# Addresses of the matrix-product operands: one distance modulo 256 bytes between what streams and what is loaded, by padded blocks and unused bytes

## The chip, the cores and the metric

One core of one Trainium2 chip runs the whole kernel in one launch. The metric is the device time in microseconds. An execution is a fixed program on five engines: PE (matrix products), ACT, DVE and POOL (element-wise work), and SP, which in this kernel issues most of the DMAs. On PE a matrix product is two records: a weight load (PEld), which puts 128 columns of the stationary operand into the array, and the matmul itself (PE), which streams the moving operand past them.

## The reference

```
h  = x + softmax_attention(layernorm(x) @ wqkv) @ wo      # 2048 x 512, 32 heads of 16
z  = gelu(layernorm(h) @ w_in)                            # 2048 x 1376
z1, z2 = z[:, :688], layernorm(z[:, 688:])
g  = w_sp @ z2 + b_sp[:, None]                            # 2048 x 2048 by 2048 x 688
out = h + (z1 * g) @ w_out                                # 688 x 512
```

All of it is float32 in and out. S is 2048, D is 512, FH is 688, FC = FH // 2 is 344.

## The kernel before

Nearly every product is made in three passes over a number split in two parts (`hi` and `lo`, both of type F32R): `mm3` issues `hi*hi`, `hi*lo` and `lo*hi` one behind the other into one PSUM accumulator, which are the lines L85, L86 and L87 of the profile. In a PE row the first name behind the arrow is the operand that streams, the second the one that is loaded: in `acc<-xT,wqk` xT streams and wqk is loaded, in `acc<-wv,xT` wv streams and xT is loaded, in `g<-t,ws` (and `g<-b,ws`, `g<-n,ws`) a block of z2 streams and a block of w_sp, `ws`, is loaded, in `acc<-wi,hT` wi streams, in `acc<-wo,o` wo, in `acc<-wu,pT` wu.

The kernel has four stages. Within each the order on PE, ACT, DVE and SP is written out by hand, from the last three stages on POOL's too.

1. **Projections.** x is normalised and transposed to `xT`; `proj_v` (wv streams, 512 columns) and `proj_qk` (xT streams, 512 columns) make v, q and k, which go to DRAM. From the fourth group of the second block on, five matmuls of the row maxima (`max_pair`, L214) stand inside each `proj_qk`.
2. **Attention.** Eight head groups; for each, 16 key blocks by 4 query blocks. PE makes scores (L647), row maxima of later rows (L214) and the weighted sum (L658); ACT takes the exponential; DVE takes the maxima. The keys `kst` of even head groups lie in a pool at one end of the memory, those of odd ones in a pool at the other end. Meanwhile `load_weights` brings wo and w_in in through a staging tile `wg` and POOL splits them into `wo2` and `wi2`.
3. **Mid stage.** For each of 16 row blocks: `make_h` (wo streams, 512 columns), `turn` (transposes into hT), and four calls of `make_z`, one for each quarter of w_in, 12 matmuls of 344 columns each, then gelu and layernorm. `gate_z` also makes the four blocks `t3`, `t2`, `n4` and `t1` of combinations of z2, each 8 by 344 numbers in a partition.
4. **Final stage.** w_sp @ z2 by seven block products of half the size in place of eight (as Strassen and Winograd have it). Each `product` is 24 matmuls of 344 columns (8 blocks by three passes). Four products for each of 8 row blocks p first (g7, g6, g4, g5), whose sums `q` go to DRAM, then three for each p (g1, g3, g2), the gate, the transposes `tp<-ident,pr` and the last product (wu streams, 512 columns, 18 matmuls for each output block).

Blocks that stream in the stages 3 and 4 are rows of 344 numbers that lie end to end:

```
wi2 = [ec.tile([P, DB, 2 * FH], F32R, name=f"wi{i}") for i in range(2)]
T = {n: [zc.tile([P, HB, FC], F32R, name=f"{n}_{i}") for i in range(2)]
     for n in ("t3", "t2", "n4", "t1")}
```

344 numbers are 1376 bytes, that is 5 * 256 + 96. A loaded block is 128 numbers, 512 bytes. So with each step to the next row the start of what streams moves by 96 bytes against the start of what is loaded, modulo 256. Tiles are put into memory one behind the other, from the left end or (side="right") from the right end, in the order in which their pools are opened; sizes are rounded up to 32 bytes.

Of the kernel before, what the change touches and what calls it, by code (L numbers as in the profile page):

```python
# [8 lines left out]
F32 = mybir.dt.float32  # L9
F32R = mybir.dt.float32r  # L10
# [8 lines left out]
P = 128  # L19
S = 2048  # L20
D = 512
H = 32
DH = 16
FH = 688
# [3 lines left out]
HB = NB // 2  # L28
NQ = S // 512
DB = D // P  # L30
# [7 lines left out]
VW = DH + 1  # L38
FB = [min(i * P, FH - P) for i in range(6)]
FC = FH // 2  # L40
LOW = -3.0e38


@with_exitstack
def block_kernel(ctx: ExitStack, tc: tile.TileContext, x, wqkv, wo, w_in, w_sp4, b_sp, w_out, out):
# [7 lines left out]
    nc = tc.nc  # L53
    E = mybir.EngineType

    const = ctx.enter_context(tc.tile_pool(name="const", bufs=1))
# [2 lines left out]
    make_identity(nc, ident)  # L59
    bias = const.tile([P, NB], F32, name="bias")  # L60
    nc.gpsimd.dma_start(bias, b_sp)

    q_scr = dram.tile([2, H * DH, S], F32, name="q_scr")
    k_scr = dram.tile([2, H * DH, S], F32, name="k_scr")
# [72 lines left out]
    qst, mx, turned = {}, {}, {}  # L137
# [118 lines left out]

    with ExitStack() as pre:
        p2 = pre.enter_context(tc.tile_pool(name="pre_2", bufs=2))
        pc = pre.enter_context(tc.tile_pool(name="pre_c", bufs=1))
        pt = pre.enter_context(tc.tile_pool(name="pre_pt", bufs=2, space=PSUM))  # L260
        ps = [pre.enter_context(tc.tile_pool(name=f"pre_ps{i}", bufs=2 - i, space=PSUM))
# [182 lines left out]
        with tc.manual_schedule(engines={E.PE, E.Activation, E.DVE, E.SP}):  # L444
# [43 lines left out]
            for g in range(3):  # L488
                a, b = 4 * g, 4 * g + 4
# [44 lines left out]
            for j in range(24):  # L534
                b, n, i = 1 + j // 8, j // 2 % 4, 1 - j % 2
# [28 lines left out]
    wc = late.enter_context(tc.tile_pool(name="wc", bufs=1))  # L564
    e2 = late.enter_context(tc.tile_pool(name="early_2", bufs=2))
    early = ctx.enter_context(ExitStack())
    ec = early.enter_context(tc.tile_pool(name="early_c", bufs=1))
    wo2 = [wc.tile([P, DB, D], F32R, name=f"wo{i}", tag=f"w{1 + i}") for i in range(2)]
    wi2 = [ec.tile([P, DB, 2 * FH], F32R, name=f"wi{i}") for i in range(2)]
    wo4 = wo.rearrange("(a p) c -> p a c", p=P)  # L570
    wi4 = w_in.rearrange("(a p) c -> p a c", p=P)

# [56 lines left out]
    with ExitStack() as at:  # L629
# [43 lines left out]

        def load_weights(i):

            t = wc.tile([P, DB * D], F32, name="wg", tag="w0")
            if i < 2:
                t = t[:, :2 * D].rearrange("p (a c) -> p a c", a=2)
                a, f = slice(2 * i, 2 * i + 2), slice(0, D)
                src, dst = wo4, wo2  # L680
            else:
                t = t[:, :2 * FH].rearrange("p (a c) -> p a c", a=2)
                b = FH * (i // 4)
                a, f = slice(i % 2 * 2, i % 2 * 2 + 2), slice(b, b + FH)
                src, dst = wi4, wi2
            nc.sync.dma_start(t, src[:, a, f])
            split(dst[0][:, a, f], dst[1][:, a, f], t, "pool", "pool")
# [134 lines left out]
    with ExitStack() as mid:  # L822
        m2 = mid.enter_context(tc.tile_pool(name="mid_2", bufs=2))
        zs, zst = {}, {}
        ph = mid.enter_context(tc.tile_pool(name="mid_ph", bufs=1, space=PSUM))
        pt = mid.enter_context(tc.tile_pool(name="mid_pt", bufs=2, space=PSUM))
        ps = mid.enter_context(tc.tile_pool(name="mid_ps", bufs=5, space=PSUM))

        def turn(sb):
# [11 lines left out]

        def make_z(sb, i, c):

            hT, f = hTs[sb], slice(i * FH + c * FC, i * FH + (c + 1) * FC)
# [81 lines left out]

    with ExitStack() as fin:
        bc = fin.enter_context(tc.tile_pool(name="fin_b", bufs=1, side="right"))
        fs = fin.enter_context(tc.tile_pool(name="fin_s", bufs=1, side="right"))
        fq = fin.enter_context(tc.tile_pool(name="fin_q", bufs=1, side="right"))  # L930
        f1 = late.enter_context(tc.tile_pool(name="fin_1", bufs=2))
# [36 lines left out]
        for p in range(HB):  # L968
            nxt, new, last = {}, [old[2], old[3], now[0], now[1]], p + 1 == HB
            ahead = p + 2 if p + 2 < HB else None  # L970
            g7, g6, g4, g5 = [next_g() for _ in range(4)]
            p6, p67 = [f1.tile([P, FC], F32, name=n) for n in ("p6", "p67")]
            q = [(fq if last else f1).tile([P, FC], F32, name=f"q{i}") for i in range(3)]

            def keep(i, g, other):
                nc.vector.tensor_add(q[i], g, other)
# [30 lines left out]
            if not last:  # L1007
                nxt["a22"] = put(new[2], a22)

                if ahead:  # L1010
                    a11 = ask(0, 0, ahead, "xr")
                else:
                    s2 = half("s4", "xr", 3)
                    for n in range(2):
                        nc.sync.dma_start(s2[n], cut(s_scr[0])[n])
                a22 = ask(1, 1, ahead, "o") if ahead else ask(0, 1, 0, "o")
            else:

                b22 = [zc.tile([P, HB, FC], F32R, name="b22", tag=f"t3_{i}") for i in range(2)]
                b21 = []  # L1020

                def put_next(b, k):
                    put_b(b, k, bs.pop(0))
                    if asked:
                        bs.append(load_b(*asked.pop(0)))

                for k in range(6):
                    put_next(b22, k)
                combine(nc.vector, s2, a22, s2, ALU.subtract)
                s4 = put(f[1], s2)  # L1030
                for k in range(6, HB):
                    put_next(b22, k)
# [3 lines left out]
            if not last:  # L1036
                nxt["s1"] = put(new[3], a21)
                if ahead:
                    a21 = a
                else:  # L1040
                    a11 = a
                b = load_b(0, 0, p + 1)
                if not ahead:
                    asked = [(1, 1, k) for k in range(HB)] + [(1, 0, k) for k in range(HB)]
                    bs = [load_b(*asked.pop(0)) for _ in range(5)]
            else:
                a12 = put(f[2], a22)
                b21 = [zc.tile([P, HB, FC], F32R, name="b21", tag=f"t2_{i}") for i in range(2)]
# [16 lines left out]
            keep(1, g4, p67)  # L1065
            product(g5, ops["s1"], T["t1"])
            if last:
                t = zc.tile([P, HB * FC], F32, name="qz", tag="t1_1")
# [11 lines left out]
        t = zc.tile([P, HB * FC], F32R, name="wu5", tag="t1_0")  # L1080
        for i, places in enumerate([[w[:, 2 * i:2 * i + 2, :] for w in wu] for i in range(2)]
                                   + [[w[:, 4, :] for w in wu], [t[:, j * D:(j + 1) * D] for j in range(2)]]):
            parts(*places, raw_u[i])
# [157 lines left out]
```

## Time and profile before

| | |
|---|---|
| median of 3 runs | 1884.37 us (1884.22 to 1887.94) |
| the profiled execution: its time, its span | 1884.14 us, 1882.3 us |
| granted PE clock | 1.00 |
| PE busy in the span | 1870.1 us, 99% |
| matmuls in the profile | 11606 |

How to read it: the span goes from the first to the last instruction; 1.8 us of the execution lie around it. A matmul's record has a modelled end and overlaps the record of the next one, so the length of a record is not what it costs. What it costs is the distance from its start to the start of the next: where rows of the timeline follow each other without a wait, the first start, the last start and the count give the mean cost of one.

### The profile page before, as it was taken

Reading aid. Unit: us, or ns where it says so; the run is one execution under the profiler, and the core shown is the slowest. Engines: PE = TensorE matmul, PEld = TensorE weight load, DVE = VectorE, ACT = ScalarE, POOL = GpSimd, SP = SyncE. Lnnn points to the kernel's source line nnn. Section 1 sums busy time; section 2 is a strip of 40 time slices with the busy share of each in tenths; the row PEclk is TensorE's granted clock in tenths of the full one; section 3 lists DMA queues with packets and bytes.
Section 4 is the critical chain, followed back from the end, with each engine's and each line's share of the span. In section 5 each row is a group of like instructions: output and inputs, shape, how many; then the busy total and the mean of one; then the engine's idle time right before and its main releaser. Section 6 shows DMA issues by size and latency. Waiting matters only on the chain.

```text
span 1882.3 us, 32332 instructions
## 1 busy us (share of the span) xinstructions
PE 1870.1 (99%) x11606; PEld 1066.4 (57%) x11606; DVE 1526.9 (81%) x3044; ACT 1328.3 (71%) x1716; POOL 205.6 (11%) x288
## 2 busy tenths in 40 slices
PE   9999999999999999999999999999999999999999
PEld 6766444444444444444444444444438999999998
DVE  6487999999999999999999999999935666867554
ACT  3334888888888888888888888888885444434221
POOL 2130000011010100000000000000001756001111
PEclk9999999999999999999999999999999999999999
DMA  6677210221120111021012011100024555768562
GB/s 190 177 199 187 51 24 25 51 54 28 38 53 18 52 41 24 19 47 38 13 38 41 16 38 38 24 13 16 4 73 129 159 160 168 222 194 269 186 190 85
DMA packets 148392, 159.82 MB, mean 85 GB/s; under 512 B 62984, under 2 KB 93208, under 8 KB 146696
## 3 DMA queue, kind: packets, MB, share of 16 engines
q1 hardware_dynamic: 143448, 146.35, 28.8%
q10 hardware_dynamic: 4752, 11.41, 1.6%
q8 instruction: 91, 1.49, 0.3%
q14 instruction: 69, 0.57, 0.1%
q0 software_dynamic: 32, 0.01, 0.0%
HBM read 101.16 MB, written 55.61 MB: 83 GB/s over the span
## 4 chain that ended last, share of the span: by engine, by line
PE 96%; DMA 1%; DVE 1%; issue 1%; ACT 0%; SPq 0%; POOLq 0%; DVEq 0%; ACTq 0%
PE pv L658 27%; PE m L214 26%; PE s L647 13%; PE acc L85 6%; PE acc L87 6%; PE acc L86 6%; PE g L87 3%; PE g L85 3%; PE g L86 3%; PE tp L1125 0%; PE tp L834 0%; DMA h<-h_scr 0%; DMA a<-in_w_sp 0%; PE tp L214 0%; PE tp L355 0%
## 5 line engine op out<-in xcount | busy, mean ns | idle before, releaser
L650 ACT ACTIVATE pt<-s 128x1024 f32<-128x1024 f32 x1024 | 993.6, 1031 | 147.5 <-PE s L647 142.0
L219 DVE TENSOR_REDUCE mx<-m 128x1 f32<-128x512 f32 x1511 | 958.8, 684 | 106.9 <-PE m L214 67.3
L214 PE MATMUL m<-kst,qst 48*128 48x512 f32 x1511 | 607.5, 448 | 0.0
L658 PE MATMUL pv<-pt,vst 128*32 128x512 f32 x4096 | 550.2, 605 | 0.7 <-ACT o L665 0.7
L647 PE MATMUL s<-qst,kst 50*128 50x512 f32 x2048 | 466.2, 428 | 2.1 <-DVE part L82 1.5
L214 PEld LDWEIGHTS m<-kst,qst 48*128 48x128 f32 x1511 | 263.5, 184 | 315.8 <-DVE mx L219 221.6
L647 PEld LDWEIGHTS s<-qst,kst 50*128 50x128 f32 x2048 | 223.0, 185 | 57.1 <-ACT pt L650 31.4
L214 PE MATMUL m<-uvs,qst 48*128 48x512 f32 x503 | 249.1, 496 | 0.0
L214 PEld LDWEIGHTS m<-uvs,qst 48*128 48x128 f32 x503 | 91.8, 183 | 207.3 <-DVE mx L219 205.3
L228 DVE CUSTOM_DVE_ANT_0 ab<-m,ab 128x512 f32<-128x512 f32 x252 | 171.7, 681 | 4.0 <-PE m L214 2.1
L658 PEld LDWEIGHTS pv<-pt,vst 128*32 128x32 f32 x4096 | 82.9, 108 | 160.3 <-issue 154.6
L224 ACT ACTIVATE ab<-m 128x512 f32<-128x512 f32 x251 | 151.0, 602 | 16.5 <-PE m L214 16.2
L79 POOL CAST mparts<-nm 128x16 fp32r<-128x16 f32 x32 | 6.3, 198 | 911.1 <-DVE nm L234 911.1
L777 ACT ACTIVATE ws<-a 128x512 fp32r<-128x512 f32 x80 | 45.9, 622 | 54.3 <-PE g L87 27.6
L85 PE MATMUL acc<-wi,hT 128*128 128x344 f32 x256 | 83.1, 325 | 0.0
L87 PE MATMUL acc<-wi,hT 128*128 128x344 f32 x256 | 81.8, 319 | 0.0
L86 PE MATMUL acc<-wi,hT 128*128 128x344 f32 x256 | 81.7, 319 | 0.0
L849 ACT ACTIVATE z<-acc 128x344 f32<-128x344 f32 x64 | 29.2, 458 | 62.7 <-PE acc L87 56.0
L778 DVE TENSOR_TENSOR ws<-a,ws 128x512 fp32r<-128x512 f32 x80 | 56.6, 750 | 13.5 <-ACT ws L777 13.4
L85 PE MATMUL g<-b,ws 128*128 128x344 f32 x192 | 62.6, 326 | 0.0
L87 PE MATMUL g<-b,ws 128*128 128x344 f32 x192 | 61.3, 319 | 0.0
L85 PE MATMUL g<-t,ws 128*128 128x344 f32 x192 | 61.3, 319 | 0.0
(193 smaller groups left out, 2134.5 us busy)
## 6 DMA issues: line engine op xcount, KB each, us to landing
a<-in_w_sp SPq DMA_DIRECT2D x80, 256.0 KB
qst<-q_scr SPq DMA_DIRECT2D x192, 64.0 KB
kst<-k_scr SPq DMA_DIRECT2D x48, 256.0 KB
z_scr<-z ACTq DMA_DIRECT2D x32, 344.0 KB
k_scr<-part SPq DMA_DIRECT2D x16, 512.0 KB
q_scr<-part SPq DMA_DIRECT2D x16, 512.0 KB
z<-z_scr SPq DMA_DIRECT2D x14, 344.0 KB
b<-z_scr SPq DMA_DIRECT2D x24, 172.0 KB
```

The source lines that it names most:

```text
L85: nc.tensor.matmul(ps, lh, rh, start=first, stop=False)
L86: nc.tensor.matmul(ps, lh, rl, start=False, stop=False)
L87: nc.tensor.matmul(ps, ll, rh, start=False, stop=last)
L214: nc.tensor.matmul(acc, q[r, p, c], keys[r, p], start=True, stop=True)
L219: nc.vector.reduce_max(at(t, e if t else e - 1), acc, axis=AX.X)
L224: nc.scalar.activation(ab[0], acc, AF.Abs)
L228: nc.vector.tensor_tensor_reduce(ab[0], acc, ab[0], 0.5, LOW, ALU.add, ALU.max, at(0, 0))
L647: nc.tensor.matmul(s[:, t, :], k[r, p, kb * P:(kb + 1) * P], q[r, p, :], start=True, stop=True)
L650: nc.scalar.activation(t, s, AF.Exp, scale=DH ** -0.5)
L658: nc.tensor.matmul(pv[0][32 * j:32 * j + 32, :], vst[hg % 2][:, c:c + 32], pts[j % 2][:, j // 2, :], start=kb == 0, stop=kb == NB - 1)
L777: nc.scalar.activation(hi, src, AF.Copy)
L778: (nc.gpsimd if el == "pool" else nc.vector).tensor_sub(lo, src, hi.bitcast(F32))
```

## The change

It moves operands in memory and leaves the arithmetic, and the order of the instructions on PE, ACT, DVE and SP, as they are. The number that it sets is, for each kind of product, (address of the first byte that streams - address of the first byte that is loaded) modulo 256. In the two built programs:

| product | matmuls, columns | before | after |
|---|---|---|---|
| xT streams, wqk loaded | 384, 512 | 192 | 0 |
| wv streams, xT loaded | 192, 512 | 0 | 0 |
| wo streams, o loaded | 192, 512 | 0 | 0 |
| wi streams, hT loaded | 768, 344 | 0, 32, ... 224, 96 of each | 0 |
| t3, t2, n4, b11, b22, b21 stream, ws loaded | 1152, 344 | 0, 32, ... 224, an eighth each, moving by 96 from block to block | 64 |
| t1 streams, ws loaded | 192, 344 | the same | 64 and 192 in turn |
| wu streams, pT loaded | 288, 512 | 224 | 0 |
| scores, odd head groups (even: 0 in both) | 1024, 512 | 160 | 192 |
| maxima, odd head groups (even: 0 in both) | 1024, 512 | 96 | 64 |

The weighted sum of the attention (L658) has every multiple of 4 equally often in both.

To this end rows of 344 numbers get a pitch of 384 (1536 bytes, 6 * 256), those of t1 a pitch of 352; unused tiles (`gap`) of 224 and 64 bytes shift what follows; `wu` starts 16 numbers into its tile. To make room, and to place it, hT moves from its own double-buffered pool into one tile in the slot `w2` (as two halves taken in turn), wo2 goes to `w0` and `w1` and the staging tile to `w2`; p6, p67, q and one each of the two h and pr tiles of the final stage have one buffer in place of two. POOL splits w_in in pieces of one row (8 conversions and 8 subtractions in place of 4 and 4).

```diff
+PITCH = 384
+    def gap(pool, size):
+        if size:
+            pool.tile([P, size // 4], F32, name="gap")
+    gap(const, 224)
...
         p2 = pre.enter_context(tc.tile_pool(name="pre_2", bufs=2))
+        pg = pre.enter_context(tc.tile_pool(name="pre_g", bufs=1))
+        gap(pg, 64)
...
-    wo2 = [wc.tile([P, DB, D], F32R, name=f"wo{i}", tag=f"w{1 + i}") for i in range(2)]
-    wi2 = [ec.tile([P, DB, 2 * FH], F32R, name=f"wi{i}") for i in range(2)]
+    wo2 = [wc.tile([P, DB, D], F32R, name=f"wo{i}", tag=f"w{i}") for i in range(2)]
+    wi2 = [ec.tile([P, DB, 4, PITCH], F32R, name=f"wi{i}")[:, :, :, :FC] for i in range(2)]
...
-            t = wc.tile([P, DB * D], F32, name="wg", tag="w0")
+            t = wc.tile([P, DB * D], F32, name="wg", tag="w2")
...
+                for j in range(2):
+                    d = slice(a.start + j, a.start + j + 1)
+                    split(wi2[0][:, d, f], wi2[1][:, d, f], t[:, j:j + 1], "pool", "pool")
...
-    T = {n: [zc.tile([P, HB, FC], F32R, name=f"{n}_{i}") for i in range(2)]
+    NARROW = FC + 8
+    def quarter(pool, name, tag, pitch=PITCH):
+        return pool.tile([P, HB, pitch], F32R, name=name, tag=tag)[:, :, :FC]
+    T = {n: [quarter(zc, n, f"{n}_{i}", NARROW if n == "t1" else PITCH) for i in range(2)]
...
+        hT = wc.tile([P, 2, 2, DB, P], F32R, name="hT", tag="w2")
...
-            hTs[sb] = [m2.tile([P, DB, P], F32R, name=f"hT{i}") for i in range(2)]
+            hTs[sb] = [hT[:, i, turned[0] % 2] for i in range(2)]
+            turned[0] += 1
...
+        gap(fin.enter_context(tc.tile_pool(name="fin_g", bufs=1, side="right")), 64)
...
-        b11 = [bc.tile([P, HB, FC], F32R, name=f"b11_{i}") for i in range(2)]
+        b11 = [quarter(bc, "b11", f"b11_{i}") for i in range(2)]
...
-            p6, p67 = [f1.tile([P, FC], F32, name=n) for n in ("p6", "p67")]
-            q = [(fq if last else f1).tile([P, FC], F32, name=f"q{i}") for i in range(3)]
+            p6, p67 = [f1.tile([P, FC], F32, name=n, bufs=1) for n in ("p6", "p67")]
+            q = [fq.tile([P, FC], F32, name=f"q{i}") for i in range(3)]
...
-        wu = [zc.tile([P, HB * FC], F32R, name="wu", tag=f"n4_{i}")[:, :5 * D].rearrange(
+        off = 16
+        wu = [zc.tile([P, HB * PITCH], F32R, name="wu", tag=f"n4_{i}")[:, off:off + 5 * D].rearrange(
...
-            h = [f2.tile([P, D], F32, name=f"h{i}") for i in range(2)]
+            h = [f2.tile([P, D], F32, name=f"h{i}", bufs=2 - i) for i in range(2)]
...
-            top, bot = [Out(p + HB * i, h[i], f2.tile([P, FH], F32, name=f"pr{i}"))
+            top, bot = [Out(p + HB * i, h[i], f2.tile([P, FH], F32, name=f"pr{i}", bufs=2 - i))
```

More of the change, by code (lines that the diff above doesn't have):

```diff
@@ L674, in load_weights @@
         def load_weights(i):
-            t = wc.tile([P, DB * D], F32, name="wg", tag="w0")
+            t = wc.tile([P, DB * D], F32, name="wg", tag="w2")
+            a = slice(i % 2 * 2, i % 2 * 2 + 2)
             if i < 2:
                 t = t[:, :2 * D].rearrange("p (a c) -> p a c", a=2)
-                a, f = slice(2 * i, 2 * i + 2), slice(0, D)
-                src, dst = wo4, wo2
+                nc.sync.dma_start(t, wo4[:, a, :])
+                split(wo2[0][:, a, :], wo2[1][:, a, :], t, "pool", "pool")
             else:
                 t = t[:, :2 * FH].rearrange("p (a c) -> p a c", a=2)
[L683 to L687, printed above, removed]
+                b = i // 4
+                nc.sync.dma_start(t, wi4[:, a, FH * b:FH * b + FH])
+                t = t.rearrange("p a (b c) -> p a b c", b=2)
+                f = slice(2 * b, 2 * b + 2)
+                for j in range(2):
+                    d = slice(a.start + j, a.start + j + 1)
+                    split(wi2[0][:, d, f], wi2[1][:, d, f], t[:, j:j + 1], "pool", "pool")
         units = [(hg, qb, kb) for hg in range(HG) for qb in range(NQ) for kb in range(NB)]
@@ L827, in block_kernel @@
         ps = mid.enter_context(tc.tile_pool(name="mid_ps", bufs=5, space=PSUM))
+        turned = [0]
         def turn(sb):
@@ L842, in make_z @@
         def make_z(sb, i, c):
-            hT, f = hTs[sb], slice(i * FH + c * FC, i * FH + (c + 1) * FC)
+            hT, f = hTs[sb], 2 * i + c
             acc = ps.tile([P, 512], F32, name="acc")
@@ L1017, in block_kernel @@
             else:
-                b22 = [zc.tile([P, HB, FC], F32R, name="b22", tag=f"t3_{i}") for i in range(2)]
+                b22 = [quarter(zc, "b22", f"t3_{i}") for i in range(2)]
                 b21 = []
@@ L1047, in block_kernel @@
                 a12 = put(f[2], a22)
-                b21 = [zc.tile([P, HB, FC], F32R, name="b21", tag=f"t2_{i}") for i in range(2)]
+                b21 = [quarter(zc, "b21", f"t2_{i}") for i in range(2)]
                 for k in range(HB):
@@ L1067, in block_kernel @@
             if last:
-                t = zc.tile([P, HB * FC], F32, name="qz", tag="t1_1")
+                t = zc.tile([P, HB * NARROW], F32, name="qz", tag="t1_1")
                 first = (t[:, :3 * FC].rearrange("p (i c) -> p i c", c=FC),
@@ L1076, in block_kernel @@
         nc.sync.dma_start(first[1][0], z_scr[0][:P, :])
-        wu = [zc.tile([P, HB * FC], F32R, name="wu", tag=f"n4_{i}")[:, :5 * D].rearrange(
+        off = 16
+        wu = [zc.tile([P, HB * PITCH], F32R, name="wu", tag=f"n4_{i}")[:, off:off + 5 * D].rearrange(
             "p (a c) -> p a c", c=D) for i in range(2)]
-        t = zc.tile([P, HB * FC], F32R, name="wu5", tag="t1_0")
+        t = zc.tile([P, HB * NARROW], F32R, name="wu5", tag="t1_0")[:, off:]
         for i, places in enumerate([[w[:, 2 * i:2 * i + 2, :] for w in wu] for i in range(2)]
```

## The prediction

> **What bounds the kernel now.** I read the page first: busy times, then the chain of work that ended last.
>
> ```profile
> PE 1870.1 (99%) x11606; PEld 1066.4 (57%) x11606; DVE 1526.9 (81%) x3044; ACT 1328.3 (71%) x1716; POOL 205.6 (11%) x288
> PE 96%; DMA 1%; DVE 1%; issue 1%; ACT 0%; SPq 0%; POOLq 0%; DVEq 0%; ACTq 0%
> ```
>
> PE carries 96% of the chain. So a change that only alters what one matmul costs reaches the end of the kernel, where PE has no other reason to wait. The busy time by stretches (columns: length, then busy time and records of PE, PEld, DVE, ACT, POOL) tells where that is: the second half of the projections, the attention, the mid stage, the products of the final stage, its end.
>
> ```profile
> 94.00:174.00 80.00, 78.79 (x343) 54.57 (x341) 61.48 (x112) 24.47 (x43) 18.19 (x21) 1.00 0.75 196
> 174.00:1418.00 1244.00, 1242.43 (x8125) 509.75 (x8125) 1108.97 (x2110) 1096.77 (x1302) 51.94 (x114) 1.00 0.16 36
> 1418.00:1574.00 156.00, 155.05 (x919) 143.84 (x918) 102.42 (x338) 66.47 (x115) 78.98 (x90) 1.00 0.52 155
> 1574.00:1718.00 144.00, 144.00 (x922) 144.00 (x921) 110.85 (x208) 62.94 (x123) 11.37 (x14) 1.00 0.66 207
> 1718.00:1882.00 164.00, 160.33 (x907) 145.78 (x906) 92.96 (x145) 44.49 (x82) 27.80 (x22) 1.00 0.52 174
> ```
>
> In the fourth stretch PE is busy all 144.00 us and DVE, the next, 110.85: a matmul that gets cheaper there shortens the kernel by as much. Projections, mid stage and end are nearly as full. The attention is not so clear: DVE and ACT are each busy for about 1100 of 1244 us.
>
> The fourth stretch holds nothing but matmuls of 344 columns. Two of its 922 records reach in from before (a record is twice as long as the distance of starts), so one costs 144.00 / 920 = 156.5 ns.
>
> **What the operands' distance does in this trace.** The kernel before already has products at several distances, so the timeline can be asked. Rows are start, length, line. First wv at distance 0, 512 columns, right behind transposes, and then farther on without a break:
>
> ```profile
> 53.28 0.39 PE L86 MATMUL acc<-wv,xT 128*128 128x512 f32 x1
> ...
> 55.59 0.39 PE L87 MATMUL acc<-wv,xT 128*128 128x512 f32 x1
> 55.82 0.39 PE L85 MATMUL acc<-wv,xT 128*128 128x512 f32 x1
> ...
> 61.03 0.39 PE L87 MATMUL acc<-wv,xT 128*128 128x512 f32 x1
> ```
>
> From 53.28 to 55.59 lie ten matmuls: 231.0 ns each. From 55.82 to 61.03 lie 23: 226.5 ns each. The first ten behind a break are uneven and dearer, then a steady state is reached. Now xT at distance 192 and wu at distance 224, also 512 columns:
>
> ```profile
> 85.98 0.40 PE L85 MATMUL acc<-xT,wqk 128*128 128x512 f32 x1
> ...
> 91.82 0.39 PE L86 MATMUL acc<-xT,wqk 128*128 128x512 f32 x1
> ```
>
> ```profile
> 1751.55 0.39 PE L85 MATMUL acc<-wu,pT 128*128 128x512 f32 x1
> ...
> 1755.52 0.40 PE L87 MATMUL acc<-wu,pT 128*128 128x512 f32 x1
> ```
>
> 25 matmuls in 5.84 us are 233.6 ns, 17 in 3.97 us are 233.5 ns, and no wait stands in either. The same shape thus costs 226.5 ns at distance 0 and 233.5 at 192 and 224: a step of 7.0 ns. From 512 and 344 columns, (226.5 - 156.5) / 168 = 0.417 ns for a column, so 344 columns alone are 143.3 ns and 13.2 ns come on top; at 192 and 224 it is 20.2 on top of 512. These 13.2 and 20.2 are what a distance can change.
>
> The Trainium skill speaks against the change here: TensorE: Matmul & The Clock Gate, Part 2 (step 1), says that PE has two independent read ports into SBUF, one for the streaming operand and one for the weight load, and that loading the next weights takes nothing from the running matmul. By that rule the gain is 0; the step of 7.0 ns speaks against it. The same page gives columns / 2.4 + 2.5 ns for a matmul behind a matmul; the trace agrees with the slope (0.417) and not with the 2.5 (13.2), and were the page's figure reached in all 2784 affected matmuls of the table, the sum would be some 34 us, as an estimate.
>
> With 344 columns no distance stays: each block moves it by 96. One product of t1, the L85 rows, one in three matmuls; the distance of the three that begin there is, in order, 32, 128, 224, 64, 160, 0, 96, 192:
>
> ```profile
> 1615.54 0.32 PE L85 MATMUL g<-t,ws 128*128 128x344 f32 x1
> ...
> 1616.95 0.31 PE L85 MATMUL g<-t,ws 128*128 128x344 f32 x1
> ...
> 1617.41 0.32 PE L85 MATMUL g<-t,ws 128*128 128x344 f32 x1
> ...
> 1617.89 0.32 PE L85 MATMUL g<-t,ws 128*128 128x344 f32 x1
> ...
> 1618.36 0.32 PE L85 MATMUL g<-t,ws 128*128 128x344 f32 x1
> ...
> 1619.30 0.32 PE L85 MATMUL g<-t,ws 128*128 128x344 f32 x1
> ```
>
> The rows span 24 matmuls in 3.76 us, three of them 0.47 on average. The three at distance 64 take 0.46 (1616.95 to 1617.41), those at 160 0.48, those at 0 0.47, the last two triples (96 and 192) 0.94 together. So 64 is the cheapest single one and 0 is average, but a triple here carries over what the one before left behind, as the ten dear matmuls above do. No row shows 344 columns at a distance that stays.
>
> **The change part by part.**
>
> *xT, 192 to 0, 384 matmuls.* The first 11 groups (132 matmuls) come two groups of 12 at a time, so (10 x 231.0 + 14 x 226.5) / 24 = 228.4 in place of 233.6: 132 x 5.2 = 0.7 us. In the other 21 groups five row maxima stand inside each group, so six matmuls follow each other and all are in the dear beginning: 231.0, 252 x 2.6 = 0.7 us. DVE is busy 61.48 of 80 us there and hides it. Together -1.4 us; ends 0 and -2.7 (all at 226.5).
>
> *wu, 224 to 0, 288 matmuls.* Groups of 18: (10 x 231.0 + 8 x 226.5) / 18 = 229.0 in place of 233.5, -1.3 us; ends 0 and -2.0.
>
> *The final products, all eight distances to 64, 1248 matmuls, and t1 half at 64 and half at 192.* The nearest rows are the triples: 0.46 against 0.47, at most 3.3 ns for one matmul, at least nothing at their resolution of 10 ns. I take 2.0 ns: 1248 x 2.0 = -2.5 us. The ends come from the step seen at 512 columns, since a distance that stays can settle a step below or above the average: 1344 x 7.0 = 9.4 us either way.
>
> *wi, all eight to 0, 768 matmuls.* The triple at 0 is the average one (0.47 / 3 = 156.7 against 156.5), and at 512 columns distance 0 also has just the 13.2 ns that 344 columns have now. I take 0; ends 768 x 7.0 = 5.4 us either way.
>
> *wv and wo* stay at 0: nothing.
>
> *Attention, odd head groups, 160 to 192 and 96 to 64.* The first scores of three head groups, the first an odd one:
>
> ```profile
> 330.64 0.52 PE L647 MATMUL s<-qst,kst 50*128 50x512 f32 x2
> ...
> 486.73 0.52 PE L647 MATMUL s<-qst,kst 50*128 50x512 f32 x2
> ...
> 642.96 0.53 PE L647 MATMUL s<-qst,kst 50*128 50x512 f32 x2
> ```
>
> The odd group takes 156.09 us and the even one, at distance 0, 156.23. A distance is worth 0.14 us for a whole group, so four odd groups bound it by 0.6 us either way; I take 0.
>
> *Fewer buffers and other slots.* DVE writes a pair of q:
>
> ```profile
> 1619.50 0.94 DVE L976 TENSOR_TENSOR q<-g,p 128x344 f32<-128x344 f32 x2 [0.47 <-PE g L87]
> ...
> 1634.53 0.94 DVE L976 TENSOR_TENSOR q<-g,p 128x344 f32<-128x344 f32 x2 [3.24 <-PE g L87]
> ```
>
> With one buffer the second write waits for the store of the first, issued 15.03 us earlier; behind it on DVE would queue the splits of the next blocks, on which PE waits. The cover is those 15 us. p6 and p67 are read at the end of one p and written again two products later, pr and h of the lower half half a p later; SP, which would hold the later loads behind h, issues it after the sum that frees it. hT in `w2` ends where a22 is put there, and on ACT the last gelu, which waits for the same matmuls, stands ahead of that. POOL's eight extra instructions lie in the attention, where it is busy 51.94 of 1244 us. All this is 0; if a cover were gone, a microsecond or two at each p, up to 10 us.
>
> *Sum.* -1.4 - 1.3 - 2.5 = -5.2 us against the profiled execution, 1884.14: 1878.9. The median of the runs lies 0.2 above that, so 1879.1.
>
> **The rivals.** *Nothing to gain (0.20).* What sets the cost may be how a matmul follows the one before (the dear ten behind a break point there), the distance being only part of it; then xT and wu gain the little that their long groups allow, the products nothing: 1882 to 1885, say 1884. For it: over eight distances 344 columns vary by no more than 0.02 us in three. Against it: 7.0 ns, steady, in three long rows. By the skill's rule of two ports, it would be this one.
>
> *A whole step down in the products (0.18).* A distance that stays lets the streams settle in one pattern, and 64, the cheapest triple, could settle a step lower: 1248 x 7.0 = 8.7, with xT and wu 11.4 us: 1873. For it: at 512 columns the levels are a step apart with nothing between. Against it: no row below 13.2 ns on top over a long run.
>
> *A step up (0.12).* The same settling, on the wrong side: today the 344-column products run over all distances and average out; at one that stays they may settle where 512 columns settle at 192 and 224, 20.2 ns on top. All 2112 of them: +14.8 - 2.7 = +12.1 us, 1896.5; wi alone: +5.4 - 5.2, no change. It is slower by over 0.2% once the average over all 2112 rises by 3.0 ns ((3.8 + 2.7) us / 2112). For it: a row of 344 columns ends at another place modulo 256 than one of 512, so a distance good for one need not be so for the other; t1 gets 192, the bad one of xT. Against it: the triples at 0 and 64 are not among the dear ones.
>
> **How the numbers follow.** The forecast has 0.50, its own range 1876 to 1882 (the products between 0 and 3.3 ns, xT and wu between half and all of their gain). The range 1872 to 1886 takes in the lower step and the case without gain and leaves out the step up. A measurement of this kernel can tell about 0.2% from no change, 3.8 us. Below 1880.6: most of the forecast (0.43) and the step down (0.18), 0.62 with a little of the rest. Within 0.2%: the case without gain and what is left of the forecast, 0.26. Slower: 0.12.
>
> **What would show it.** In the profile after, xT's long groups at 226.5 to 229 ns from start to start and wu's groups at 229; 344-column matmuls in the stretch with full PE at 154 to 155 ns in the mean, and now with equal triples within one product; wi at 156.7; head groups at 156.1 to 156.3 us; DVE not waiting for a store ahead of q. The prediction is wrong if wu stays at 233.5, if the products stand a whole step off (near 150 or 163), or if a wait for a DMA comes into the chain in the last two stages.

## The result, and the profile after

| | before | after |
|---|---|---|
| median of 15 runs each, us | 1885.74 (1883.51 to 1887.94) | 1881.88 (1880.59 to 1884.46) |
| ratio, 95% interval | | 0.9980 (0.9972 to 0.9988), that is -3.9 us (-5.3 to -2.3) |
| the profiled execution: time, span, us | 1884.14, 1882.3 | 1882.25, 1880.5 |

The changed kernel is faster by 3.9 us, where 5.2 were forecast. The two profiled executions lie only 1.9 us apart: the profile before is 1.6 us under the median of its kernel, the one after 0.4 above. So the traces are used for the cost of single steps, the runs for the whole.

In the kernel after, the lines of `mm3` are L93, L94 and L95. First its busy times and the chain that ended last, then the same five stretches, each moved by what the start of its stage moved:

```profile
PE 1867.3 (99%) x11606; PEld 1065.3 (57%) x11606; DVE 1526.9 (81%) x3044; ACT 1328.3 (71%) x1716; POOL 206.5 (11%) x296
...
PE 95%; DMA 2%; DVE 1%; ACT 1%; issue 0%; POOL 0%; SPq 0%; DVEq 0%; POOLq 0%; ACTq 0%
```

```profile
94.00:173.00 79.00, 77.36 (x342) 54.15 (x340) 61.62 (x112) 24.45 (x43) 18.18 (x21) 1.00 0.78 199
173.00:1416.50 1243.50, 1242.20 (x8125) 509.16 (x8128) 1108.68 (x2109) 1096.98 (x1302) 52.85 (x122) 1.00 0.16 36
1416.50:1572.50 156.00, 155.15 (x920) 144.15 (x914) 103.33 (x338) 66.38 (x115) 79.74 (x90) 1.00 0.53 156
1572.50:1716.00 143.50, 143.50 (x921) 143.50 (x920) 109.38 (x205) 62.89 (x123) 10.49 (x14) 1.00 0.66 202
1716.00:1880.50 164.50, 158.84 (x907) 145.23 (x905) 93.73 (x148) 44.30 (x82) 27.94 (x22) 1.00 0.54 177
```

Projections and products got shorter, the mid stage did not, and the last stretch has the same matmuls in 0.5 us more, with PE busy 1.5 us less: PE now waits there. By the marks of the two traces (first scores, first wi, first product, first wu matmul, last matmul) the kernel after is ahead by 1.26, 1.73, 1.59, 0.95 and 1.87 us: what the products gain is lost again before the first wu matmul.

Now the timeline after, in the order of the prediction's rows: xT, one whole wu group, a pair of q, the first scores of head groups 1, 2 and 3.

```profile
85.73 0.39 PE L93 MATMUL acc<-xT,wqk 128*128 128x512 f32 x1
...
91.62 0.39 PE L95 MATMUL acc<-xT,wqk 128*128 128x512 f32 x1
...
1751.20 0.39 PE L93 MATMUL acc<-wu,pT 128*128 128x512 f32 x1
...
1755.08 0.40 PE L95 MATMUL acc<-wu,pT 128*128 128x512 f32 x1
...
1632.77 0.94 DVE L999 TENSOR_TENSOR q<-g,p 128x344 f32<-128x344 f32 x2 [3.23 <-PE g L95]
...
329.36 0.46 PE L657 MATMUL s<-qst,kst 50*128 50x512 f32 x1
...
485.33 0.47 PE L657 MATMUL s<-qst,kst 50*128 50x512 f32 x1
...
641.54 0.47 PE L657 MATMUL s<-qst,kst 50*128 50x512 f32 x1
```

26 xT matmuls in 5.89 us are 226.5 ns each, 17 of wu in 3.88 us are 228.2 (before: 233.6 and 233.5). The pair of q waits for PE, not for a store. The odd head group takes 155.97 us, the even one 156.21.

Where the new wait is, the rows tell from the last splits of b to the first transposes; first before, then after:

```profile
1710.22 0.95 ACT L777 ACTIVATE b<-b 128x344 fp32r<-128x344 f32 x2 [1.61 <-DMA b<-z_scr]
...
1716.87 1.06 DVE L1160 SCALAR_TENSOR_TENSOR pr<-g,bias,qz 128x344 f32<-128x344 f32 x2 [0.41 <-DMA qz<-g_scr]
1717.96 0.87 DVE L1164 TENSOR_TENSOR pr<-pr,qz 128x688 f32<-128x688 f32 x1
...
1719.85 0.82 PE L1125 MATMUL tp<-ident,pr 128*128 128x128 f32 x6
```

```profile
1709.93 0.96 ACT L795 ACTIVATE b<-b 128x344 fp32r<-128x344 f32 x2 [2.39 <-DMA b<-z_scr]
...
1716.79 1.06 DVE L1184 SCALAR_TENSOR_TENSOR pr<-g,bias,qz 128x344 f32<-128x344 f32 x2 [0.60 <-DMA qz<-g_scr]
1717.88 0.88 DVE L1188 TENSOR_TENSOR pr<-pr,qz 128x688 f32<-128x688 f32 x1
...
1718.86 0.84 PE L1149 MATMUL tp<-ident,pr 128*128 128x128 f32 x6 [0.93 <-issue]
...
1730.76 0.50 PE L95 MATMUL acc<-wu,pT 128*128 128x512 f32 x1 [0.85 <-DVE pT L90]
```

Before, `pr` is ready at 1718.83 and PE comes for it at 1719.85: 1.02 us to spare. After, PE would be there some 1 us before `pr` is ready at 1718.76. Such a chain (loads of b, their splits on ACT and DVE, the last sums q, their store and reload as qz, pr) is called **the way** below; it is counted from the start of the last t3 product, which is followed by 162 matmuls up to the transposes. It was 25.38 us long before (1694.47 to 1719.85, set by PE) and is 26.37 after (1692.49 to 1718.86). A second wait stands before the second group of wu; before it was 0.3 us. That it follows from the same lateness is not shown: the kernel with each at its cheapest, below, has it too (PE idle for 0.48 us, here 0.85), though its transposes start on time.

### The profile page after: what moved, and what is told of

Read it like the earlier page. It is cut to its first block, busy times and chain, and to the rows that moved or that the text cites. A ratio compares the mean times of both kernels' runs of the same rounds, so it can differ in the third digit from the quotient of the medians.

```text
span 1880.5 us, 32358 instructions
## 1 busy us (share of the span) xinstructions
PE 1867.3 (99%) x11606; PEld 1065.3 (57%) x11606; DVE 1526.9 (81%) x3044; ACT 1328.3 (71%) x1716; POOL 206.5 (11%) x296
## 4 chain that ended last, share of the span: by engine, by line
PE 95%; DMA 2%; DVE 1%; ACT 1%; issue 0%; POOL 0%; SPq 0%; DVEq 0%; POOLq 0%; ACTq 0%
PE pv L668 27%; PE m L222 26%; PE s L657 13%; PE acc L93 6%; PE acc L95 6%; PE acc L94 5%; PE g L93 3%; PE g L95 3%; PE g L94 3%; PE tp L1149 0%; DMA kst<-k_scr 0%; DMA b<-z_scr 0%; DMA a<-in_w_sp 0%; PE tp L855 0%; PE acc L440 0%
## 5 line engine op out<-in xcount | busy, mean ns | idle before, releaser
L668 PEld LDWEIGHTS pv<-pt,vst 128*32 128x32 f32 x4096 | 82.9, 108 | 159.7 <-issue 153.4
L93 PE MATMUL acc<-wi,hT 128*128 128x344 f32 x256 | 83.2, 325 | 0.0
L95 PE MATMUL acc<-wi,hT 128*128 128x344 f32 x256 | 81.9, 320 | 0.0
L94 PE MATMUL acc<-wi,hT 128*128 128x344 f32 x256 | 81.3, 318 | 0.0
L93 PE MATMUL g<-b,ws 128*128 128x344 f32 x192 | 62.5, 325 | 0.0
L93 PE MATMUL g<-t,ws 128*128 128x344 f32 x192 | 61.2, 319 | 0.0
L95 PE MATMUL g<-b,ws 128*128 128x344 f32 x192 | 61.1, 318 | 0.0
```

The lines of the kernel that those rows point to most:

```text
L93: nc.tensor.matmul(ps, lh, rh, start=first, stop=False)
L94: nc.tensor.matmul(ps, lh, rl, start=False, stop=False)
L95: nc.tensor.matmul(ps, ll, rh, start=False, stop=last)
L668: nc.tensor.matmul(pv[0][32 * j:32 * j + 32, :], vst[hg % 2][:, c:c + 32], pts[j % 2][:, j // 2, :], start=kb == 0, stop=kb == NB - 1)
```

## The experiments

The costs below are mean distances from start to start in the traces, in the 11th and later matmuls of an uninterrupted series unless another count is named.

**Other distances (four scans).** Each is the changed kernel with other gaps; only addresses move. This is scan1:

```diff
-    gap(const, 224)
+    gap(const, 96)
...
-        gap(pg, 64)
+        gap(pg, 96)
...
+    gap(ec, 64)
     wi2 = [ec.tile([P, DB, 4, PITCH], F32R, name=f"wi{i}")[:, :, :, :FC] for i in range(2)]
...
-        gap(fin.enter_context(tc.tile_pool(name="fin_g", bufs=1, side="right")), 64)
+        gap(fin.enter_context(tc.tile_pool(name="fin_g", bufs=1, side="right")), 192)
```

The other three have, in the same places, 160, 128, 192, 128 / 32, 160, 128, 0 / 128, 192, 96, 160, and wu's offset at 40, 40 and 8 numbers.

> The changed kernel with other distances that stay: wi at 64 (was 0), the final products at 192 (was 64; t1 at 192 and 64 in turn), xT at 32 (was 0), wu at 128 (was 0). Theory A (at a distance that stays, the starts settle in a pattern that belongs to the distance and the column count): wi takes 156.0 ns from start to start, what the products at 64 take in the changed kernel; the products at 192 about 153.7; xT and wu leave 226.7, for 230 to 234. Theory B (the distance is incidental, what counts is how long a group runs without a break): xT and wu stay at 226.7 and 228, wi at 157.8 and the products at 156.0.

> As before with wi at 192, the products at 128 (t1 at 128 and 0), xT at 64, wu at 160. Theory A: wi at 192 takes what the products at 192 take in the run before, to 0.3 ns, about 153.7; the products at 128 about 158; xT and wu above 226.7. Theory B: nothing differs from the changed kernel (157.8, 156.0, 226.7, 228).

> As before with wi at 128, the products at 0 (t1 at 0 and 128), xT at 96, wu at 32. Theory A: wi at 128 takes what the products at 128 take in the run before (about 158), the products at 0 what wi at 0 takes in the changed kernel (157.8); wu at 32 what xT at 32 takes. Theory B: nothing differs (157.8, 156.0, 226.7, 228).

> As before with wi at 96, the products at 160 (t1 at 160 and 32), xT at 128, wu at 64. Theory A: the products at 160, the dearest triple of the kernel before, are the slowest of all, about 160; wi at 96 about 157; wu at 64 and xT at 128 take what xT at 64 and wu at 128 take in the runs before. Theory B: nothing differs (157.8, 156.0, 226.7, 228).

One run each: 1884.73, 1886.69, 1886.54 and 1886.56 us, beside 1886.12 of the kernel before. Two of the four were granted 0.998 of the PE clock, so these times rank nothing; the traces give the costs:

| distance | 0 | 32 | 64 | 96 | 128 | 160 | 192 | 224 |
|---|---|---|---|---|---|---|---|---|
| 512 columns, xT, ns | 226.6 | 233.1 | 229.0 | 233.3 | 232.2 | | 233.0 | |
| 512 columns, wu, ns | 226.6 | 233.1 | 229.0 | | 232.6 | 234.3 | | 233.2 |
| 344 columns, t3, t2, n, ns | 153.3 | | 156.0 | | 157.1 | 160.0 | 157.7 | |
| 344 columns, wi, ns | 157.8 | | 155.2 | 157.7 | 157.2 | | 158.1 | |

(0 and 192 of xT, 0 and 224 of wu, 64 of the products and 0 of wi are the kernels before and after; with all eight distances mixed, before, the products cost 156.8 and wi 157.4.) Where xT and wu stood at the same distance they cost the same to 0.4 ns, in different stages, tiles and kernels. So with 512 columns theory A holds, B falls, and 0 is the cheapest of the eight. With 344 columns the two rows agree at 128 and 192 and not at 0 and 64: a distance does not give the cost alone. The 153.7 that scan1 expected for the products at 192 was a miss (157.7), and so was the 157.8 that scan3 expected for those at 0 (153.3).

A stretch of products without a wait shows how far apart they are (columns as above; before, after, then the scans at 0 and at 160; two of the records reach in from before):

```profile
1594.00:1714.00 120.00, 120.00 (x768) 120.00 (x767) 94.58 (x169) 52.03 (x103) 0.53 (x1) 1.00 0.67 207
```

```profile
1594.00:1714.00 120.00, 120.00 (x771) 120.00 (x770) 93.82 (x168) 50.99 (x101) 0.53 (x1) 1.00 0.68 208
```

```profile
1594.00:1714.00 120.00, 120.00 (x781) 120.00 (x780) 93.88 (x168) 50.34 (x102) 0.53 (x1) 1.00 0.67 211
```

```profile
1594.00:1714.00 120.00, 120.00 (x754) 120.00 (x753) 91.72 (x165) 49.43 (x100) 0.53 (x1) 1.00 0.66 206
```

120 / 766, 769, 779 and 752 are 156.7, 156.0, 154.0 and 159.6 ns for all products, t1 with them.

**The 512-column part alone**, on the kernel before:

```diff
         p2 = pre.enter_context(tc.tile_pool(name="pre_2", bufs=2))
+        pre.enter_context(tc.tile_pool(name="pre_g", bufs=1)).tile([P, 16], F32, name="gap")
...
-        wu = [zc.tile([P, HB * FC], F32R, name="wu", tag=f"n4_{i}")[:, :5 * D].rearrange(
+        wu = [zc.tile([P, HB * FC], F32R, name="wu", tag=f"n4_{i}")[:, 8:8 + 5 * D].rearrange(
...
-        t = zc.tile([P, HB * FC], F32R, name="wu5", tag="t1_0")
+        t = zc.tile([P, HB * FC], F32R, name="wu5", tag="t1_0")[:, 8:]
```

> The kernel before with nothing but xT at distance 0 (64 unused bytes ahead of the constants of the projections) and wu at distance 0 (8 numbers into its tile); the 344-column products keep all eight distances, all buffers stay. Theory A (each distance has its own settled cost, and the parts add up): xT from 233.1 to 228.7 ns and wu from 233.0 to 228.0 as in the changed kernel, together 384 x 4.4 + 288 x 5.0 = 3.1 us at most where nothing else waits, 2.9 us by the stage marks: about 1882.9 beside 1885.8 of the kernel before, so most of the changed kernel's -3.9 us. Theory C (the gain comes from the other slots, buffers or the 344 columns): less than 1 us of it here.

1882.36 against 1886.64 us in the same series: 0.9977 (0.9968 to 0.9986), -4.3 us (-6.0 to -2.6). In its trace:

```profile
85.53 0.39 PE L85 MATMUL acc<-xT,wqk 128*128 128x512 f32 x1
...
91.42 0.39 PE L87 MATMUL acc<-xT,wqk 128*128 128x512 f32 x1
...
1717.76 0.82 PE L1126 MATMUL tp<-ident,pr 128*128 128x128 f32 x6
```

26 matmuls in 5.89 us again, and no wait ahead of the transposes (way 25.37 us). `pr` is ready there 0.34 us before PE comes for it, so the 1.02 us to spare in the profile before are no fixed amount:

```profile
1716.55 0.87 DVE L1165 TENSOR_TENSOR pr<-pr,qz 128x688 f32<-128x688 f32 x1
```

Two small edits bring all that the whole change brings. Theory A.

**The rest alone**: the changed kernel with xT back at 192 and wu at 224.

```diff
-        gap(pg, 64)
+        gap(pg, 0)
...
-        off = 16
+        off = 8
```

> The changed kernel with xT back at 192 and wu back at 224; the padded rows at distance 64 and 0, the slots and the fewer buffers stay. Theory A: products 156.6 to 156.0 ns (1344 x 0.6 = -0.8 us), wi 157.4 to 157.8 (768 x 0.4 = +0.3 us), perhaps a stall of up to 1 us more ahead of the last products: between -1 and +0.5 us beside the kernel before, about 1885. Theory C: 2 to 4 us faster, like the changed kernel.

1885.07 against 1886.64: 0.9991 (0.9982 to 0.9999), -1.6 us (-3.4 to -0.2), rather more than expected (in its trace the attention is 0.9 us shorter, 1093.81 to 1092.91) and well under 4. Products 156.0, wi 157.7 as in the changed kernel, and its waits are there too (columns: total us, times, longest):

```profile
PE tp L1149 <- issue: 1.0, 1, 1.0
PE acc L95 <- DVE pT L90: 0.9, 1, 0.9
```

**The changed kernel again.**

> The changed kernel itself once more, for its time on the same chip as the other three and for a second profile. If the stalls of 1.09 us ahead of the first transposes of the last products and of 1.01 us between the first two wu groups belong to the change, they stand here again at the same places; if they are of one execution, they are gone and the time is the same to 1 us. Levels: xT 228.7, wu 228.0, wi 157.8, products 156.0 ns.

1882.20 us, 0.9973 (0.9963 to 0.9983). xT 228.5 and wu 228.1 on average, wi 157.7, products 156.0 as in the first profile; the two waits stand at the same places, 1.68 and 1.56 us. They belong to the change.

**Other slots and fewer buffers alone**, on the kernel before, nothing padded:

```diff
-    wo2 = [wc.tile([P, DB, D], F32R, name=f"wo{i}", tag=f"w{1 + i}") for i in range(2)]
+    wo2 = [wc.tile([P, DB, D], F32R, name=f"wo{i}", tag=f"w{i}") for i in range(2)]
...
+        hT = wc.tile([P, 2, 2, DB, P], F32R, name="hT", tag="w2")
...
-            p6, p67 = [f1.tile([P, FC], F32, name=n) for n in ("p6", "p67")]
-            q = [(fq if last else f1).tile([P, FC], F32, name=f"q{i}") for i in range(3)]
+            p6, p67 = [f1.tile([P, FC], F32, name=n, bufs=1) for n in ("p6", "p67")]
+            q = [fq.tile([P, FC], F32, name=f"q{i}") for i in range(3)]
...
-            h = [f2.tile([P, D], F32, name=f"h{i}") for i in range(2)]
+            h = [f2.tile([P, D], F32, name=f"h{i}", bufs=2 - i) for i in range(2)]
...
-            top, bot = [Out(p + HB * i, h[i], f2.tile([P, FH], F32, name=f"pr{i}"))
+            top, bot = [Out(p + HB * i, h[i], f2.tile([P, FH], F32, name=f"pr{i}", bufs=2 - i))
```

> The kernel before with only the other slots and the fewer buffers of the changed kernel (hT in w2, wo2 in w0 and w1, p6, p67, q and one each of h and pr with one buffer); no padding, every product at its distances of before, wu at 224 again by 16 unused numbers. The question is the stall ahead of the first transposes of the last products (1.09 and 1.68 us in the two profiles of the changed kernel, 1.14 with the 344-column part alone, none before and none with the 512-column part alone) and the one between the first wu groups (1.0 to 1.6 us against 0.2 to 0.3). Theory G (the buffers make the way from the last t3 product to the first transposes longer): both stalls stand here too, or the way grows from 25.4 to over 26 us, and the time is 1 to 2 us above the kernel before. Theory H (the way has its own length, set by the loads of the b blocks, and becomes visible as the products get shorter): no stall over 0.4 us at either place, 25.4 us, time within 0.5 us of the kernel before, about 1885.8.

1886.78 against 1886.01: 1.0005 (0.9997 to 1.0014), +0.8 us (-0.6 to +2.6). The products cost 156.6 on average as before, and yet:

```profile
1703.71 0.49 ACT L777 ACTIVATE b<-b 128x344 fp32r<-128x344 f32 x1 [1.79 <-DMA b<-z_scr]
...
1722.19 0.84 PE L1129 MATMUL tp<-ident,pr 128*128 128x128 f32 x6 [0.71 <-issue]
```

The way is 26.25 us (1695.94 to 1722.19) and PE starts the transposes 0.88 us late; the wait between the wu groups is there with 0.72. So theory G: the waits come with the slots and buffers, at products as dear as before. In the kernels with the new buffers the way, where PE waited at its end, was from 25.8 to 27.5 us long; in the two with the old ones PE never waited there. The first step at which these three traces part is a load of b that is issued 2.80 us behind the start of the last t3 product in all of them; its split on DVE starts at 7.29 us before, at 8.30 here, at 8.16 after. But the buffers alone do not decide that load: in scan1, scan2, scan4 and the kernel with each at its cheapest (below), which have the same ones, the split starts at 6.98 to 7.16. In the last of these four, whose way begins at 1691.45:

```profile
1698.52 0.52 DVE L797 TENSOR_TENSOR b<-b,b 128x344 fp32r<-128x344 f32 x1 [0.33 <-ACT b L796]
```

What all twelve traces with the new buffers share comes later: ACT takes the last block of b 3.2 to 3.6 us behind the issue of its load, and `pr` is ready 25.65 to 27.43 us into the way. In the two traces with the old buffers (the kernel before, the 512-column part) it is 2.4 us, and 24.36 and 25.03. Theory G rests on these two against twelve. Why the loads land later, and which of the buffers does it, was not tried. In time the cost is not told from nothing.

**Each at its cheapest**: the changed kernel with wi at 64 and the products at 0 (t1 at 0 and 128).

```diff
-    gap(const, 224)
+    gap(const, 32)
...
+    gap(ec, 64)
     wi2 = [ec.tile([P, DB, 4, PITCH], F32R, name=f"wi{i}")[:, :, :, :FC] for i in range(2)]
...
-        gap(fin.enter_context(tc.tile_pool(name="fin_g", bufs=1, side="right")), 64)
+        gap(fin.enter_context(tc.tile_pool(name="fin_g", bufs=1, side="right")), 0)
...
-        off = 16
+        off = 32
```

> The changed kernel with wi at distance 64 in place of 0 and the final products at 0 in place of 64 (t1 at 0 and 128 in turn); xT and wu at 0 as there. Each at the cheapest level that the four scans showed. Theory A: wi 157.8 to 155.2 ns (768 x 2.6 = -2.0 us), the products 156.0 to 153.35 (1152 x 2.65 = -3.1 us), t1 156.0 to 156.6 (+0.1 us): 5 us below the changed kernel, about 1877, 9 below the kernel before. Theory D (the level of a 344-column stream depends on what ran ahead of it as much as on its own distance, since wi and the products differ at the same distance): the levels of the scans don't come together in one kernel, and the gain over the changed kernel is 2 us or less.

1879.54 us, 0.9963 (0.9951 to 0.9976), -7.0 us: the fastest of all, 2.7 below the changed kernel of the same series, not the 5 of theory A (the intervals of the two overlap). wi costs 156.0; but t3, t2 and n cost 157.7, where the scan had 153.3 with **the same addresses** of every product, to the byte. Theory D is right on that, though the gain of 2 us or less that it gave was passed. This trace holds both values at one address; b behind the transposes, then behind 18 matmuls of wu:

```profile
1734.96 0.32 PE L94 MATMUL g<-b,ws 128*128 128x344 f32 x1
...
1736.54 0.32 PE L95 MATMUL g<-b,ws 128*128 128x344 f32 x1
...
1740.94 0.32 PE L94 MATMUL g<-b,ws 128*128 128x344 f32 x1
...
1742.93 0.32 PE L95 MATMUL g<-b,ws 128*128 128x344 f32 x1
```

Ten in 1.58 us are 158 ns each, thirteen in 1.99 us 153.1.

**What selects the pattern.** Three kernels with the products at the same addresses: wi at 128 as in the scan, nine idle matmuls of 512 columns ahead of the first product (below), and one in place of nine.

```diff
+                warm, w_s2 = ps_o.tile([P, 512], F32, name="acc"), ops["s2"][0]
+                for i in range(9):
+                    nc.tensor.matmul(warm, w_s2[:, 0, :], w_s2[:, :4, :], start=i == 0, stop=i == 9 - 1)
                 for blocks in (range(HB - 1), range(HB - 1, HB)):
```

> As the kernel with everything at its cheapest, but wi at distance 128 in place of 64, so that the products are entered as in the scan where they ran at 153.3 ns; the addresses of the products are the same in all three kernels, xT and wu stay at 0. Theory E (at one and the same addresses a 344-column stream has two settled patterns, 153.3 and 157.8 ns, and what ran ahead selects one): products at 153.3 again, wi at 157.2; against the kernel with wi at 64, 768 x 1.2 = +0.9 us for wi and (576 + 72) x 4.4 = -2.9 us for t3, t2, n and the first b products: about 2 us faster, 1877.5. Theory F (the two levels are a difference from one execution to the next): either level, no relation to wi; about 1880.

> As the kernel with everything at its cheapest (wi at 64), with nine matmuls of 512 columns at distance 0, whose result nobody reads, ahead of the first final product. In the trace of that kernel the b products run at 158 ns behind transposes and at 153 behind wu's 18 matmuls of 512 columns at distance 0, at the same addresses. Theory E: behind the nine the t3 product begins at 153 and all products up to the first transposes stay there: 648 x 4.4 = -2.9 us, less 9 x 0.23 = 2.0 us for the nine, about 1 us faster. Theory F, or a level set by the addresses: 157.7 as before and 2 us slower.

> The same with one such matmul in place of nine. Theory E: one matmul of another length shifts the entry, and the products settle at one of the two levels; at 153.3 the kernel is 2.9 - 0.2 = 2.7 us faster than without it, at 157.8 it is 0.2 us slower; nothing between. Which of the two isn't told by the runs so far. A mean between the two levels, steady, would contradict it.

With wi at 128 the products run at 153.3, with nine idle matmuls at 153.3, with one at 157.7, none at a mean between: theory E, and F falls. The b products bear it out: in all five traces with the products at 0 each of six series behind wu settles at 153.3 or 153.4 ns (in scan3 too, where wu stood at 32), and the last series, behind transposes, at 157.8 or 157.9. So both costs stand in every one of these executions.

But the time does not follow. 1883.06 (0.9984, 0.9976 to 0.9993), 1883.70 (0.9991, 0.9982 to 1.0) and 1882.28 (0.9983, 0.9974 to 0.9992), so none is faster than the kernel with the dearer products (0.9963, five runs of another series), where 2 and 1 us were expected of the first two. The third should have been 0.2 us slower than that kernel and is 3.8 us slower by the ratios. Not all of this is the products': in the traces the two kernels with idle matmuls are already 2.2 and 1.4 us behind it at the first wi, and up to there they do not differ from it. With wi at 128, and with the nine:

```profile
1594.00:1714.00 120.00, 120.00 (x781) 120.00 (x780) 94.39 (x169) 51.28 (x102) 0.53 (x1) 1.00 0.68 208
...
1709.66 1.01 ACT L796 ACTIVATE b<-b 128x344 fp32r<-128x344 f32 x2 [2.55 <-DMA b<-z_scr]
...
1719.04 1.30 PE L1150 MATMUL tp<-ident,pr 128*128 128x128 f32 x5 [2.45 <-issue]
```

```profile
1594.00:1714.00 120.00, 120.00 (x781) 120.00 (x780) 91.52 (x164) 48.85 (x99) 0.52 (x1) 1.00 0.66 206
...
1721.88 0.85 PE L1153 MATMUL tp<-ident,pr 128*128 128x128 f32 x6 [2.25 <-issue]
```

The products end earlier and PE waits some 2.5 us for `pr`: the way is 27.53 and 27.34 us long, PE's work in it 24.9. From the first product to the first transposes lie 834 matmuls:

| kernel | products (t3, t2, n), ns | these 834, us | the way, us |
|---|---|---|---|
| before | 156.8 | 130.63 | 25.38, no wait |
| scan3 | 153.3 | 130.52 | 26.91 |
| wi at 128 | 153.3 | 131.14 | 27.53 |
| nine idle matmuls | 153.3 | 130.93 | 27.34 |
| each at its cheapest | 157.7 | 131.62 | 25.77 |
| one idle matmul | 157.7 | 133.10 | 27.19 |
| scan4 (at 160) | 160.0 | 133.22 | 25.89, no wait |

At 160 the dearer products are paid in full (834 x 3.1 ns = 2.6 us). Cheaper ones are paid up to the last t3 product: the 672 matmuls ahead of it take 103.6 us in the three kernels at 153.3 and 105.26 before. The way takes it back. Why it is so long there, and why one idle matmul makes it 1.4 us longer at the same price, was not found; and no kernel has the old buffers with products at 153.3, so whether they would have kept the gain is open.

With wi at 128 more than the wait was lost. Behind it:

```profile
1720.64 0.49 PE L94 MATMUL g<-b,ws 128*128 128x344 f32 x1
...
1722.07 0.50 PE L93 MATMUL acc<-wu,pT 128*128 128x512 f32 x1
```

```profile
1719.00:1722.00 3.00, 2.96 (x12) 2.99 (x13) 1.50 (x3) 1.33 (x3) 0.93 (x1) 0.50 0.96 310
```

The granted PE clock is 0.50 in these 3 us, five matmuls take 286 ns each, and from the first transposes to the first wu matmul 3.03 us pass, where it is 1.63 with the nine, whose wait of 2.25 us left the clock at 1.00.

## Why the prediction was right, and where it was not

Direction and size held: 1879.1 us forecast, 1881.88 measured, within 1872 to 1886; -5.2 against -3.9 us (-5.3 to -2.3). That the sum was met so nearly is in part luck: the products gave a third of their term, and waits that stood at nothing took 1.8 us. The runs also gained 2.1 us more than the two traces, and that part can't be given to a step. The steps, by the two traces (added up: -1.8 us, as the spans have it):

| step | forecast, us | measured | from |
|---|---|---|---|
| xT | -1.4 | -1.7 | 233.1 to 228.7 ns on average, 384 |
| wu | -1.3 | -1.4 | 233.0 to 228.0, 288 |
| products | -2.5 | -0.8 | 156.6 to 156.0, 1344 |
| wi | 0 | +0.3 | 157.4 to 157.8, 768 |
| attention | 0 | -0.4 | 1093.81 to 1093.45 us from the first scores to those of the eighth head group |
| buffers and slots | 0 | +1.8 | 1.1 us ahead of the transposes, 0.7 more between the wu groups |
| the rest | not in the sum | +0.4 | 0.3 of it at the first wv |

*xT and wu* went as worked out: a steady row of 226.5 behind a dearer beginning. The rows of xT are longer than they were taken to be: twelve follow each other between the maxima, not six (17 series of 12), and 180 of the 384 stand in series of 24 or 42, so xT gained more than its term. The 512-column part alone carries the whole gain within the intervals.

*The products* were mis-sized: 2.0 ns were taken from one triple at distance 64, 0.46 us among eight that follow each other and take 0.46 to 0.48. In the next t1 product of the same trace the triple at 64 takes 0.47:

```profile
1631.98 0.32 PE L85 MATMUL g<-t,ws 128*128 128x344 f32 x1
...
1632.45 0.32 PE L85 MATMUL g<-t,ws 128*128 128x344 f32 x1
```

The prediction itself said that a triple carries over what went before, and then used it as a price. The scans show that triples could not rank distances: 0, "average" there, settles at 153.3 or 157.8, and 160 at 160.0 steadily. Of the rival of a whole step down, 7.0 ns, about half came true for products at 0 (153.3 against 156.7), but the change puts them at 64.

*The bound.* The step "a matmul that gets cheaper there shortens the kernel by as much" fails in the kernels as they were built: DVE's 110.85 of 144 us was read as room, but what came next was not an engine's sum, it was the way from the b loads to `pr`, which had 1.02 us to spare at its end in the profile before and none with the new buffers (only the products at 160 left some). There 1.65 us that the products at 153.3 had gained became a wait.

*Fewer buffers at nothing* fails too. The cover that was named, 15 us between two writes of q, held (the pair waits for PE). The wait came at a place that was not costed: `pr` is ready 26.27 us into the way in place of 24.36. Its 1.8 us lie well inside the bound of 10 us. That the buffers do it is shown as far as the experiment with them alone goes; how is open.

*Nothing to gain* (and with it the rule of two independent ports, by the Trainium skill, TensorE: Matmul & The Clock Gate, Part 2, step 1, which would make the distance worth nothing) is refuted by 226.6 to 234.3 ns for one and the same shape. That rival's reason, that it counts how a matmul follows the one before, is right beside it for 344 columns. *A step up* did not come at 64 and 0; at 160 there is about half of one (160.0 against 156.7).

## What to carry to other kernels

Put what streams and what is loaded at a distance of 0 modulo 256 bytes where rows of 512 columns run long: here 6 to 7 ns of 233 for each, for a few unused bytes. Take no price from short mixed stretches: let a condition stand for a whole series before it is called cheap. And before a stage full of PE work is credited with a gain, look for the slack where its results are handed over; here it was 0.3 to 1 us.

## What the runs showed of the hardware that was not expected

- One 344-column stream has two settled costs at the same addresses, 153.3 and 157.8 ns (start to start 153 153 154 and 159 156 158, repeated), each found again from the first product to the transposes, though 24 matmuls of t1 at other distances come between every 72; what ran ahead selects one. Behind 128-column transposes b settled at 157.8, behind wu at 153.3.
- Distance 160 is a pattern of its own: every start 160 ns behind the last, without a spread.
- 512 columns cost 226.6 at 0, 229.0 at 64, 232.2 to 234.3 at the others that were tried, the same for xT and wu. At 0 the series had one cost; at 224 series of wu settled at 233.1 or 233.6, at 128 at 232.4 or 234.0.
- The second pattern is not a matter of distance 0 alone: wi at 64 cost 155.2 in one kernel and 156.0 in three others, and in scan1 b at 192 cost 157.8 behind wu and 160.0 behind transposes.
- A wait of 2.45 us of PE was followed by 3 us at a granted clock of 0.50 in one trace; one of 2.25 us in another was not.
- Why a distance costs what it does was not found. That the difference counts, and not the place of one operand, fits the runs: in three kernels with xT at 0 both operands lie behind 0, 32 or 224 unused bytes of the constants, and it costs 226.6 or 226.7 ns in all.
